# The last pass's sums inverted at full width, and the last tile stored in halves

## Chip, cores and metric

The kernel runs on one core of a Trainium2 chip. The metric is the device time of one execution in microseconds; lower is better. The inputs are bfloat16 and so is the output.

## What is computed

One block of attention whose output is gated, with a residual, over 2048 tokens of width 640. `x` is normalised (layer norm), and the result `xn` goes two ways:

```python
# attention: 32 heads of 20 columns
qkv = xn @ wqkv
p = softmax(q @ k.T * 20 ** -0.5)            # per head, 2048 x 2048
s = concat_heads(p @ v) @ wo
# gate: a gated pair of matrices (640 -> 1728 -> 640)
g = silu((sigmoid(xn @ w_gate) * (xn @ w_up)) @ w_down)
out = x + s * g
```

The part that matters here is the division in the softmax. The kernel does not divide the probabilities; it computes unnormalised sums `p @ v` together with the row sums of `p`, and divides the 20 columns of each head by the head's sum afterwards.

## The kernel before

**Passes.** The queries are cut into 4 chunks of 512 (`QC`), the heads into 8 groups of 4 (`NG`, `GH`). One pass handles one chunk and one group: for each of 16 key tiles and 4 heads TensorE computes a 128 x 512 block of scores (`score`, L1155), ScalarE takes the exponential of two or three blocks at once into `p` (L1177), VectorE takes that of some extra blocks by a cubic polynomial in four steps (`dve_exp`, L1188 to L1201; its scores lie in a bank named `spare`), and TensorE multiplies `p` with the values into `oacc` (`pv`, L1289). Each head has 32 rows of `oacc`: row 0 is the head's sum (the values carry a column of ones), rows 1 to 20 are its outputs.

**Order.** The order of all instructions on each engine is fixed when the program is built. A planner holds a clock for TensorE (`pe`), queues for ScalarE and VectorE (`act`, `dve`) with an assumed cost for each task, and cells that say when a result is there. Jobs are generators that ask for a free PSUM bank, emit matmuls and add VectorE tasks; two small banks (`misc0`, `misc1`, names `work` and `spare`) are shared by all jobs and by the extra score blocks. On the chip each engine runs its list in order and waits on semaphores.

**Normal division.** After an ordinary pass `normalise` copies `oacc` to `oev` (L772), sends the four sum rows through DRAM into a 128 x 16 tile `den`, inverts that (L782), sends it back through DRAM spread over each head's 32 rows (`rl`) and multiplies (L801), which gives `oT`, the operand of the output projection.

**The last pass** (chunk 3, group 7) is divided without that round trip. Its 512 queries are cut in two parts of 256 (`PARTS`), and each part's `oacc` columns are copied out as soon as they are complete (`take_part`, L815). The first part is divided in the job `last_job`, while the second part's scores still run; the second part is divided in the code at the end of the kernel, after everything else. Both do the same:

1. one matmul per 128 queries with `oev` as the stationary operand and `pick` as the moving one (L827, L1404) turns the four sums of each query into four columns; two such matmuls give 128 x 8 sums;
2. VectorE inverts the 128 x 8 values (L834, L1412) and copies each of them to 32 neighbouring columns, `rb` (L839, L1414);
3. one matmul per 128 queries with the fp32 identity `identf` (L847, L1416) turns `rb` back, so that each head's inverse stands in its 32 rows;
4. VectorE multiplies `oev` with that (L854, L1419) into `oT`.

**The output of the last chunk.** `part_job` has projected groups 0 to 5 of the last chunk beforehand, gated the result and added `x` (L751, L756; the sum with `x` by an accumulating DMA, L759), which gives `ahead`. What is left for each tile of 128 tokens are the matmuls of groups 6 and 7 (L866 for the first part, `out_mm`, L1393, for the second), a gate on each half of 320 columns (`gated`, L879, reads PSUM) and one addition of `gq_last` and `ahead` over 640 columns with the store of the tile (`summed`, L882 and L883). At the end of the kernel `keep_clock` (L1399) issues matmuls on zeros into a bank that nobody reads. The addition of the first part's last tile is kept in `later` and issued in the code at the end, behind the matmuls with `pick`. In the code at the end, gates and additions alternate: two gates and the addition of tile 2, then two gates and the addition of tile 3.

Of the kernel before, what the change touches and what calls it, by code (L numbers as in the profile page):

```python
# [9 lines left out]
FP32 = mybir.dt.float32  # L10
BF16 = mybir.dt.bfloat16
ACT = mybir.ActivationFunctionType
ALU = mybir.AluOpType
AXISX = mybir.AxisListType.X

P = 128
PARTS = ((0, 256), (256, 256))
HEAD = 32
GH = 4
NG = HEAD // GH  # L20
QC = 512
HALF = 320
# [6 lines left out]
OBUFS, WB = 1, 2  # L29
# [16 lines left out]
def kernel(  # L46
# [11 lines left out]
    nc = tc.nc  # L58
# [3 lines left out]
    S, D = x2.shape  # L62
# [6 lines left out]
    NQC = S // QC  # L69
# [7 lines left out]
    out_view = out2.rearrange("(p t) d -> p t d", t=TT)  # L77

    dram = ctx.enter_context(tc.tile_pool(name="dram", bufs=1, space=bass.MemoryType.DRAM))
    const = ctx.enter_context(tc.tile_pool(name="const", bufs=1))  # L80
# [15 lines left out]
    bound = const.tile([P, P], BF16, name="bound")  # L96
    heads = const.tile([P, DENSE, HEAD], BF16, name="heads")
    bounds = const.tile([P, DENSE, P], BF16, name="bounds")
    identf = const.tile([P, P], FP32, name="identf")
    pick = const.tile([P, GH], FP32, name="pick")  # L100
    zero = const.tile([P, P], BF16, name="zero")

    xnT = persist.tile([P, KD, S], BF16, name="xnT")
# [6 lines left out]
    wk = ctx.enter_context(tc.tile_pool(name="wk", bufs=2))  # L110
# [52 lines left out]
    with tc.tile_pool(name="setup", bufs=1) as sp, \  # L163
# [8 lines left out]
        sums = sp.tile([P, TT], FP32, name="sums")  # L172
# [183 lines left out]
        nc.gpsimd.memset(bounds, 0.0)  # L356
        nc.gpsimd.memset(v_all[:, :, VF:HEAD, 0:1], 1.0)
        nc.gpsimd.memset(wo_pad.rearrange("p g d -> p (g d)"), 0.0)
        make_identity(nc, identf)
        nc.gpsimd.memset(pick, 0.0)  # L360
        for j in range(GH):
            nc.gpsimd.memset(pick[32 * j:32 * j + 1, j:j + 1], 1.0)

    main = ExitStack()
    psum = main.enter_context(tc.tile_pool(name="psum", bufs=1, space=bass.MemoryType.PSUM,
# [6 lines left out]
    PE_OUT, SEM = 260.0, 70.0  # L372
# [37 lines left out]
    act, dve = Engine(), Engine()  # L410
    pe = [0.0]
# [38 lines left out]
    banks = [Cell(0.0), Cell(0.0)]  # L450
# [15 lines left out]
    def give_bank(held, cell):  # L466
        banks[held] = cell

    oTs, ot_cells, k_cells, q_cells, v_cells = {}, {}, {}, {}, {}
# [264 lines left out]
    gq_last, ahead = {}, []  # L734
# [72 lines left out]
    taken_parts, later = {}, []  # L807
# [11 lines left out]

    def last_job(u):  # L820
        q0, width = PARTS[u]
        part, n = taken_parts[u], width // P
        tiles = range(q0 // P, (q0 + width) // P)
        yield "wait", [part["cell"]]
        held, pd = yield "bank",
        for k in range(n):
            nc.tensor.matmul(pd[:, k * GH:(k + 1) * GH], lhsT=part["oev"][:, k * P:(k + 1) * P], rhs=pick,  # L827
                             start=True, stop=True, skip_group_check=True)
            yield "mm", 250.0, 0.0
        made = {}  # L830

        def invert():
            made["rq"] = wk.tile([P, n, GH], FP32, tag="den", bufs=2, name="rq")
            nc.vector.reciprocal(out=made["rq"].rearrange("p t j -> p (t j)"), in_=pd[:, 0:GH * n])  # L834

        def spread():
            made["rb"] = glu[0].tile([P, D], FP32, tag="gqr", bufs=4, name="rb")[:, 0:n * P].rearrange(
                "p (t j i) -> p t j i", t=n, j=GH)
            nc.vector.tensor_copy(out=made["rb"], in_=made["rq"].unsqueeze(3).to_broadcast([P, n, GH, 32]))  # L839

        cell = dve.add(160.0, [Cell(pe[0] + PE_OUT)], invert, -1)
        give_bank(held, cell)
        cell = dve.add(300.0, [cell], spread, -1)
        yield "wait", [cell]
        held, prl = yield "bank",
        for k in range(n):
            nc.tensor.matmul(prl[:, k * P:(k + 1) * P], lhsT=made["rb"][:, k, :, :].rearrange("p j i -> p (j i)"),  # L847
                             rhs=identf, start=True, stop=True, skip_group_check=True)
            yield "mm", 330.0, 200.0

        def scale():
            if steps[-1] not in oTs:
                oTs[steps[-1]] = wk.tile([P, QC], BF16, tag="oT", bufs=NG + 3, name="oT")
            nc.vector.tensor_tensor(out=oTs[steps[-1]][:, q0:q0 + width], in0=part["oev"], in1=prl[:, 0:width], op=ALU.mult)  # L854

        cell = dve.add(70.0 + width, [Cell(pe[0] + PE_OUT)], scale, -1)
        give_bank(held, cell)
        yield "known", lambda: all((NQC - 1) * 4 + t4 in out_cells for t4 in tiles)
        yield "wait", [cell, ot_cells[steps[-2]]]
        pair = glu[0].tile([P, D], FP32, tag="gqr", bufs=4, name="ot").bitcast(BF16)  # L860
        for t4 in tiles:
            got = []
            for h in range(2):
                held, ps = yield "bank",
                for g in range(NG - 2, NG):
                    nc.tensor.matmul(ps[:, 0:HALF], lhsT=oTs[NQC - 1, g][:, t4 * P:(t4 + 1) * P],  # L866
                                     rhs=wo_pad[:, g, h * HALF:(h + 1) * HALF], start=(g == NG - 2), stop=(g == NG - 1))
                    yield "mm", MM3
                got.append(dve.add(400.0, [Cell(pe[0] + PE_OUT)], lambda t4=t4, h=h, ps=ps: gated(t4, h, ps), 1))
                give_bank(held, got[-1])  # L870
            end = lambda t4=t4: summed(t4, pair[:, t4 % 2 * D:(t4 % 2 + 1) * D])
            if u == len(PARTS) - 2 and t4 == tiles[-1]:
                later.append(end)
            else:
                dve.add(740.0, [out_cells[(NQC - 1) * 4 + t4], *got], end, 2)

    def gated(t4, h, ps):
        gq = gq_last[t4][:, h * HALF:(h + 1) * HALF]
        nc.vector.scalar_tensor_tensor(out=gq, in0=ps[:, 0:HALF], scalar=0.25, in1=gq, op0=ALU.mult, op1=ALU.mult)  # L879

    def summed(t4, ot):
        nc.vector.tensor_tensor(out=ot, in0=gq_last[t4], in1=ahead[0][:, t4, :], op=ALU.add)  # L882
        nc.sync.dma_start(out=out_view[:, (NQC - 1) * 4 + t4, :], in_=ot)  # L883

    steps = [(qc, g) for qc in range(NQC) for g in range(NG)]
# [29 lines left out]
    for qc in range(NQC):  # L915
        parts = [[g for g in range(1, NG) if max(TILES[g]) == t] for t in range(5)] if not qc else [list(range(NG))]
        for groups in filter(None, parts):
            tiles = sorted({t for g in groups for t in TILES[g]})
# [8 lines left out]
    for h0, h1, n in V_PARTS:  # L927
        for t in range(0 if h0 else V_SETUP, TT, n):
            tiles = list(range(t, min(t + n, TT)))
# [20 lines left out]
    glu = []  # L950
# [363 lines left out]
    for t, a in ((4, 4 * Dh), (5, 0)):  # L1314
        for k in range(2):
            row, j = a + k * Dh, 2 * (t - 4) + k
# [3 lines left out]
    while pv_pass[0] < len(steps) - 1 + len(PARTS):  # L1320
# [5 lines left out]
        p = min(b0, NB - 1) // PER_PASS  # L1326
        until, stuck, can = 1e18, False, False
        if b0 < NB:
# [13 lines left out]
            if can and (until <= pe[0] + (0.0 if mode[0] == "score" else 40.0) or idle):  # L1342
                idle = False
                n = issue()
# [4 lines left out]
        held = sum(len(q) for q in ready_p)  # L1349
# [32 lines left out]
    qc, g = steps[-1]  # L1382
    q0, width = PARTS[-1]
    tiles = range(q0 // P, (q0 + width) // P)
    units = [(t4, h) for t4 in tiles for h in range(2)]
    oev = taken_parts[len(PARTS) - 1]["oev"]
    main.close()
    ending = ctx.enter_context(tc.tile_pool(name="ending", bufs=1, space=bass.MemoryType.PSUM))
    banks = [ending.tile([P, 512], FP32, tag=f"end{k}", name="last") for k in range(2 * QC // P)]
    banks, pd, prl, unused = banks[1:1 + len(units)], banks[6], banks[7], banks[0]  # L1390

    def out_mm(bank, t4, h, gg):
        nc.tensor.matmul(bank[:, 0:HALF], lhsT=oTs[qc, gg][:, t4 * P:(t4 + 1) * P],  # L1393
                         rhs=wo_pad[:, gg, h * HALF:(h + 1) * HALF],
                         start=(gg == NG - 2), stop=(gg == NG - 1), skip_group_check=True)

    def keep_clock(n):
        for _ in range(n):
            nc.tensor.matmul(unused, lhsT=zero, rhs=xnT[:, 0, 0:512], start=True, stop=True, skip_group_check=True)  # L1399

    for bank, (t4, h) in zip(banks[:-1], units):
        out_mm(bank, t4, h, NG - 2)
    for k, t4 in enumerate(tiles):
        nc.tensor.matmul(pd[:, k * GH:(k + 1) * GH], lhsT=oev[:, k * P:(k + 1) * P], rhs=pick,  # L1404
                         start=True, stop=True, skip_group_check=True)
    for end in later:
        end()
    out_mm(banks[-1], *units[-1], NG - 2)
    keep_clock(2)
    n = len(tiles)  # L1410
    rq = wk.tile([P, n, GH], FP32, tag="den", bufs=2, name="rq")
    nc.vector.reciprocal(out=rq.rearrange("p t j -> p (t j)"), in_=pd[:, 0:GH * n])  # L1412
    rb = wk.tile([P, n, GH, 32], FP32, tag="rl", bufs=OBUFS, name="rb")
    nc.vector.tensor_copy(out=rb, in_=rq.unsqueeze(3).to_broadcast([P, n, GH, 32]))  # L1414
    for k, t4 in enumerate(tiles):
        nc.tensor.matmul(prl[:, k * P:(k + 1) * P], lhsT=rb[:, k, :, :].rearrange("p j i -> p (j i)"), rhs=identf,  # L1416
                         start=True, stop=True, skip_group_check=True)
    keep_clock(2)
    nc.vector.tensor_tensor(out=oTs[qc, g][:, q0:], in0=oev, in1=prl[:, 0:width], op=ALU.mult)  # L1419
    pair = glu[0].tile([P, D], FP32, tag="gqr", bufs=4, name="ot").bitcast(BF16)  # L1420
    for bank, (t4, h) in zip(banks, units):
        out_mm(bank, t4, h, NG - 1)
        gated(t4, h, bank)
        if h == 1:
            summed(t4, pair[:, t4 % 2 * D:(t4 % 2 + 1) * D])
# [1 line left out]
_INS = ['A_x', 'A_wqkv', 'A_wo', 'B_x', 'B_w_gate', 'B_w_up', 'B_w_down']  # L1427
_OUTS = [((1, 2048, 640), 'bfloat16')]
# [25 lines left out]
```

## Time and profile before

| | |
|---|---|
| median of 3 runs | 894.33 us (893.8 to 894.76) |
| the profiled execution | 894.27 us, span of its instructions 892.1 us |
| ScalarE (ACT) busy | 870.6 us, 98% of the span |
| VectorE (DVE) busy | 840.7 us, 94% |
| TensorE (PE) busy | 804.6 us, 90% |
| GpSimd (POOL) busy | 162.0 us, 18% |
| granted TensorE clock, mean | 0.998 |

The span runs from the first to the last instruction; the rest of the execution's time, 2.2 us, lies around it. Start times in the views count from the start of the span. A row of the groups gives the line of the kernel, the engine, the operation, the tiles that it writes and reads with their shapes, how often it ran, its busy time in us, the mean of one in ns, and the idle time of the engine before it with what ended it. In the chain of waits each piece has its start, its length in us, the engine and the line. A VectorE operation's length reaches some 0.08 us into the next one's: 512 columns take 0.68 us and follow each other at 0.60.

### The profile page before, as it was taken

The numbers are of one execution on the slowest core, as the hardware profiler recorded it, in microseconds if no ns is written. First come the engines' busy times: TensorE is split into PE (matmuls) and PEld (weight loads), VectorE is DVE, ScalarE is ACT, GpSimd is POOL, SyncE is SP. The second block draws the span as 40 slices with busy tenths as digits, with TensorE's granted clock in tenths as the row PEclk, the third lists the DMA queues.
The fourth block names the chain that finished last, engine by engine and source line by source line (L and its number), as shares of the span: only waits on it lengthen the run. The fifth ranks groups of instructions, "written<-read, shape, count | busy, mean of one in ns | idle before, by whom it ended". The sixth has DMA issues, their size and how long they took to land.

```text
span 892.1 us, 16911 instructions
## 1 busy us (share of the span) xinstructions
PE 804.6 (90%) x6227; PEld 290.3 (33%) x6310; DVE 840.7 (94%) x1487; ACT 870.6 (98%) x837; POOL 162.0 (18%) x305
## 2 busy tenths in 40 slices
PE   5899899998999999999899998989999898999896
PEld 3344333332223333232233332223333332233333
DVE  7799999999999999997999999999999989999997
ACT  6999999999999999999999999999999999999995
POOL 7401111111111212111101221101112220111121
PEclk9999999999999999999999999999999999999999
DMA  8113231135451234223212243313113432200012
GB/s 317 46 35 90 64 109 35 52 98 150 109 133 42 64 89 69 65 59 72 64 23 79 70 81 79 71 26 77 34 45 85 108 54 70 67 17 21 14 32 71
DMA packets 107672, 64.40 MB, mean 72 GB/s; under 512 B 80350, under 2 KB 101906, under 8 KB 107498
## 3 DMA queue, kind: packets, MB, share of 16 engines
q1 hardware_dynamic: 97382, 47.21, 19.8%
q0 software_dynamic: 10208, 16.11, 8.2%
q8 instruction: 49, 0.80, 0.4%
q14 instruction: 33, 0.27, 0.1%
HBM read 50.45 MB, written 16.13 MB: 75 GB/s over the span
## 4 chain that ended last, share of the span: by engine, by line
ACT 64%; issue 18%; PE 10%; DVE 7%; DMA 0%; SPq 0%; DVEq 0%; ACTq 0%
ACT p L1177 59%; PE sc L1155 3%; ACT tnh L651 3%; PE oacc L1289 2%; DVE dy L1188 2%; PE work L644 1%; DVE du L1193 1%; PE work L124 1%; PE work L680 1%; ACT td L691 1%; DVE stats L227 1%; DVE p L1201 1%; DVE du L1197 1%; PE work L150 1%; DMA x_sb<-in_A_x_dram 0%
## 5 line engine op out<-in xcount | busy, mean ns | idle before, releaser
L1177 ACT ACTIVATE p<-sc 128x1536 bf16<-128x1536 f32 x717 | 827.9, 1358 | 2.0 <-PE oacc L1289 1.4
L1155 PE MATMUL sc<-qT,kT_all 21*128 21x512 bf16 (+1 forms) x1848 | 280.0, 375 | 57.4 <-ACT p L1177 49.3
L1188 DVE TENSOR_SCALAR dy<-spare 128x512 f32<-128x512 f32 x257 | 175.6, 683 | 22.9 <-PE spare L1155 20.2
L1155 PEld LDWEIGHTS <-kT_all 21*128 21x128 bf16 x2112 | 91.0, 91 | 286.6 <-issue 274.6
L1197 DVE SCALAR_TENSOR_TENSOR du<-du,dy 128x512 f32<-128x512 f32 x257 | 174.4, 682 | 1.7
L1201 DVE SCALAR_TENSOR_TENSOR p<-du,dy 128x512 uint16<-128x512 f32 x257 | 174.2, 680 | 1.4
L1193 DVE SCALAR_TENSOR_TENSOR du<-dy 128x512 f32<-128x512 uint16 x257 | 174.4, 682 | 0.8
L1289 PE MATMUL oacc<-p,v_all 128*21 128x512 bf16 (+1 forms) x2112 | 157.3, 376 | 0.6 <-DVE v_all L157 0.3
L1155 PE MATMUL spare<-qT,kT_all 21*128 21x512 bf16 (+1 forms) x264 | 98.6, 378 | 0.0
L773 POOL DMA_DIRECT2D den_dram<-oev x31 | 18.0, 579 | 391.5 <-DVE oev L772 391.5
L680 PE MATMUL work<-wd,hT 128*128 128x320 bf16 x448 | 85.5, 302 | 0.1
L644 PE MATMUL work<-xnT,wg 128*128 128x512 bf16 (+1 forms) x261 | 77.6, 383 | 1.9 <-issue 0.8
L657 PE MATMUL work<-xnT,wu 128*128 128x512 bf16 (+1 forms) x268 | 73.1, 381 | 1.2 <-DVE dy L1188 0.3
L789 POOL DMA_DIRECT2D rl<-rec_dram x124 | 62.0, 512 | 57.7 <-DMA rec_dram<-den 48.0
L1265 PE MATMUL oacc<-xnT,zero 128*128 128x512 bf16 x165 | 56.0, 384 | 3.4 <-issue 2.5
L1289 PEld LDWEIGHTS <-v_all 128*21 128x21 bf16 x2112 | 31.1, 90 | 62.0 <-issue 60.1
L680 PEld LDWEIGHTS <-hT 128*128 128x128 bf16 x448 | 35.0, 97 | 48.6 <-issue 39.1
L651 ACT ACTIVATE tnh<-work 128x512 bf16<-128x512 f32 (+1 forms) x56 | 41.2, 735 | 0.0
L661 DVE SCALAR_TENSOR_TENSOR hT<-tnh,work 128x512 bf16<-128x512 bf16 (+1 forms) x56 | 37.9, 678 | 2.2 <-ACT tnh L651 2.2
L783 POOL DMA_DIRECT2D rec_dram<-den x31 | 17.0, 547 | 120.0 <-DVE den L782 115.3
L719 PE MATMUL work<-wo_pad,oT 128*128 128x320 bf16 x192 | 35.6, 302 | 0.5 <-issue 0.5
L644 PEld LDWEIGHTS <-wg 128*128 128x128 bf16 (+1 forms) x280 | 21.7, 98 | 42.8 <-issue 31.1
(123 smaller groups left out, 553.6 us busy)
## 6 DMA issues: line engine op xcount, KB each, us to landing
wg<-in_B_w_gate_dram SPq DMA_DIRECT2D x52, 160.0 KB
wu<-in_B_w_up_dram SPq DMA_DIRECT2D x52, 160.0 KB
rl<-rec_dram POOLq DMA_DIRECT2D x124, 64.0 KB, 2.5
qT<-q_dram SPq DMA_DIRECT2D x31, 128.0 KB
gq_dram<-d POOLq DMA_DIRECT2D x12, 320.0 KB, 2.5
gqr<-gq_dram SPq DMA_DIRECT2D x12, 320.0 KB
kT_all<-k_dram SPq DMA_DIRECT2D x28, 128.0 KB
wd<-in_B_w_down_dram SPq DMA_DIRECT2D x13, 160.0 KB
```

The lines of the kernel that those rows point to most:

```text
L644: nc.tensor.matmul(psg[0:fsz, :], lhsT=wg[:, kd, 0:fsz], rhs=xnT[:, kd, cols], start=(kd == 0), stop=(kd == KD - 1))
L651: nc.scalar.activation(out=made["t"][0:fsz, :], in_=psg[0:fsz, :], func=ACT.Tanh, scale=0.5)
L657: nc.tensor.matmul(psu[0:fsz, :], lhsT=wu[:, kd, 0:fsz], rhs=xnT[:, kd, cols], start=(kd == 0), stop=(kd == KD - 1))
L680: nc.tensor.matmul(psd[:, 0:HALF], lhsT=hT[0:fsz, kf, t4 * P:(t4 + 1) * P], rhs=glu[1][0:fsz, kf, e0_:e1_], start=(kf == 0), stop=(kf == N ...
L789: nc.gpsimd.dma_start(out=t["rl"][32 * j:32 * j + 32, :], in_=rec_dram[n, j:j + 1, :].to_broadcast([32, QC]))
L1155: nc.tensor.matmul(ps[:, c0:c0 + n], lhsT=kT_all[rows, g, kt * P:(kt + 1) * P], rhs=qTs[qc, g][rows, q0:q0 + n], start=True, stop=True, ti ...
L1177: nc.scalar.activation(out=buf.tile(), in_=ps, func=ACT.Exp, bias=EXP_BIAS, scale=exp_scale)
L1188: nc.vector.tensor_scalar(out=t["y"], in0=ps, scalar1=LEAST, scalar2=None, op0=ALU.max)
L1193: nc.vector.scalar_tensor_tensor(out=t["u"], in0=t["f"], scalar=CUBE_2, in1=t["f"], op0=ALU.add, op1=ALU.mult)
L1197: nc.vector.scalar_tensor_tensor(out=t["u"], in0=t["u"], scalar=CUBE_1, in1=t["f"], op0=ALU.add, op1=ALU.mult)
L1201: nc.vector.scalar_tensor_tensor(out=buf.tile()[:, 0, :].bitcast(U16), in0=t["u"], scalar=CUBE_SCALE, in1=t["y"], op0=ALU.mult, op1=ALU.add)
L1289: nc.tensor.matmul(oacc[32 * j:32 * j + 1 + Dh, q0:q0 + width], lhsT=v_all[:, kt, GH * g + j, 0:1 + Dh], rhs=buf.ap[:, i, c0:c0 + width], ...
```

## The change

The four steps of the division become three in both places: one fp32 matmul with a constant `spread` (row 32j holds ones in columns 32j to 32j+31) puts each head's sum into all of its 32 rows, 128 x 256 at once; VectorE inverts these 128 x 256 values out of PSUM; VectorE multiplies with `oev`. In the planner the VectorE task of `last_job` is one task with a cost of 652 ns, in place of tasks with 160, 300 and 326 ns. In the code at the end the four gates come first and the additions after them, in halves of 320 columns: the first half of tile 2 is added by GpSimd, the other three by VectorE. Tile 2 is stored whole, tile 3 in two halves. Of the constants, `identf` and `pick` go and `spread` comes. Two times two filler matmuls (`keep_clock`) become three.

```diff
--- before.py
+++ after.py
@@ -96,8 +96,7 @@
     bound = const.tile([P, P], BF16, name="bound")
     heads = const.tile([P, DENSE, HEAD], BF16, name="heads")
     bounds = const.tile([P, DENSE, P], BF16, name="bounds")
-    identf = const.tile([P, P], FP32, name="identf")
-    pick = const.tile([P, GH], FP32, name="pick")
+    spread = const.tile([P, P], FP32, name="spread")
     zero = const.tile([P, P], BF16, name="zero")
 
     xnT = persist.tile([P, KD, S], BF16, name="xnT")
@@ -356,10 +355,9 @@
         nc.gpsimd.memset(bounds, 0.0)
         nc.gpsimd.memset(v_all[:, :, VF:HEAD, 0:1], 1.0)
         nc.gpsimd.memset(wo_pad.rearrange("p g d -> p (g d)"), 0.0)
-        make_identity(nc, identf)
-        nc.gpsimd.memset(pick, 0.0)
+        nc.gpsimd.memset(spread, 0.0)
         for j in range(GH):
-            nc.gpsimd.memset(pick[32 * j:32 * j + 1, j:j + 1], 1.0)
+            nc.gpsimd.memset(spread[32 * j:32 * j + 1, 32 * j:32 * j + 32], 1.0)
 
     main = ExitStack()
     psum = main.enter_context(tc.tile_pool(name="psum", bufs=1, space=bass.MemoryType.PSUM,
@@ -819,41 +817,21 @@
 
     def last_job(u):
         q0, width = PARTS[u]
-        part, n = taken_parts[u], width // P
+        part = taken_parts[u]
         tiles = range(q0 // P, (q0 + width) // P)
         yield "wait", [part["cell"]]
-        held, pd = yield "bank",
-        for k in range(n):
-            nc.tensor.matmul(pd[:, k * GH:(k + 1) * GH], lhsT=part["oev"][:, k * P:(k + 1) * P], rhs=pick,
-                             start=True, stop=True, skip_group_check=True)
-            yield "mm", 250.0, 0.0
-        made = {}
-
-        def invert():
-            made["rq"] = wk.tile([P, n, GH], FP32, tag="den", bufs=2, name="rq")
-            nc.vector.reciprocal(out=made["rq"].rearrange("p t j -> p (t j)"), in_=pd[:, 0:GH * n])
-
-        def spread():
-            made["rb"] = glu[0].tile([P, D], FP32, tag="gqr", bufs=4, name="rb")[:, 0:n * P].rearrange(
-                "p (t j i) -> p t j i", t=n, j=GH)
-            nc.vector.tensor_copy(out=made["rb"], in_=made["rq"].unsqueeze(3).to_broadcast([P, n, GH, 32]))
-
-        cell = dve.add(160.0, [Cell(pe[0] + PE_OUT)], invert, -1)
-        give_bank(held, cell)
-        cell = dve.add(300.0, [cell], spread, -1)
-        yield "wait", [cell]
-        held, prl = yield "bank",
-        for k in range(n):
-            nc.tensor.matmul(prl[:, k * P:(k + 1) * P], lhsT=made["rb"][:, k, :, :].rearrange("p j i -> p (j i)"),
-                             rhs=identf, start=True, stop=True, skip_group_check=True)
-            yield "mm", 330.0, 200.0
+        held, sums = yield "bank",
+        nc.tensor.matmul(sums[:, 0:width], lhsT=spread, rhs=part["oev"], start=True, stop=True)
+        yield "mm", 700.0, 500.0
 
         def scale():
             if steps[-1] not in oTs:
                 oTs[steps[-1]] = wk.tile([P, QC], BF16, tag="oT", bufs=NG + 3, name="oT")
-            nc.vector.tensor_tensor(out=oTs[steps[-1]][:, q0:q0 + width], in0=part["oev"], in1=prl[:, 0:width], op=ALU.mult)
-
-        cell = dve.add(70.0 + width, [Cell(pe[0] + PE_OUT)], scale, -1)
+            over = glu[0].tile([P, D], FP32, tag="gqr", bufs=4, name="over")[:, 0:width]
+            nc.vector.reciprocal(out=over, in_=sums[:, 0:width])
+            nc.vector.tensor_tensor(out=oTs[steps[-1]][:, q0:q0 + width], in0=part["oev"], in1=over, op=ALU.mult)
+
+        cell = dve.add(140.0 + 2 * width, [Cell(pe[0] + PE_OUT)], scale, -1)
         give_bank(held, cell)
         yield "known", lambda: all((NQC - 1) * 4 + t4 in out_cells for t4 in tiles)
         yield "wait", [cell, ot_cells[steps[-2]]]
@@ -1387,7 +1365,12 @@
     main.close()
     ending = ctx.enter_context(tc.tile_pool(name="ending", bufs=1, space=bass.MemoryType.PSUM))
     banks = [ending.tile([P, 512], FP32, tag=f"end{k}", name="last") for k in range(2 * QC // P)]
-    banks, pd, prl, unused = banks[1:1 + len(units)], banks[6], banks[7], banks[0]
+    banks, sums, unused = banks[1:1 + len(units)], banks[7], banks[0]
+
+    def total(engine, t4, h, pair):
+        cols = slice(h * HALF, (h + 1) * HALF)
+        engine.tensor_tensor(out=pair[:, t4 % 2 * D:(t4 % 2 + 1) * D][:, cols], in0=gq_last[t4][:, cols],
+                             in1=ahead[0][:, t4, cols], op=ALU.add)
 
     def out_mm(bank, t4, h, gg):
         nc.tensor.matmul(bank[:, 0:HALF], lhsT=oTs[qc, gg][:, t4 * P:(t4 + 1) * P],
@@ -1400,29 +1383,27 @@
 
     for bank, (t4, h) in zip(banks[:-1], units):
         out_mm(bank, t4, h, NG - 2)
-    for k, t4 in enumerate(tiles):
-        nc.tensor.matmul(pd[:, k * GH:(k + 1) * GH], lhsT=oev[:, k * P:(k + 1) * P], rhs=pick,
-                         start=True, stop=True, skip_group_check=True)
+    nc.tensor.matmul(sums[:, 0:width], lhsT=spread, rhs=oev, start=True, stop=True, skip_group_check=True)
     for end in later:
         end()
     out_mm(banks[-1], *units[-1], NG - 2)
-    keep_clock(2)
-    n = len(tiles)
-    rq = wk.tile([P, n, GH], FP32, tag="den", bufs=2, name="rq")
-    nc.vector.reciprocal(out=rq.rearrange("p t j -> p (t j)"), in_=pd[:, 0:GH * n])
-    rb = wk.tile([P, n, GH, 32], FP32, tag="rl", bufs=OBUFS, name="rb")
-    nc.vector.tensor_copy(out=rb, in_=rq.unsqueeze(3).to_broadcast([P, n, GH, 32]))
-    for k, t4 in enumerate(tiles):
-        nc.tensor.matmul(prl[:, k * P:(k + 1) * P], lhsT=rb[:, k, :, :].rearrange("p j i -> p (j i)"), rhs=identf,
-                         start=True, stop=True, skip_group_check=True)
-    keep_clock(2)
-    nc.vector.tensor_tensor(out=oTs[qc, g][:, q0:], in0=oev, in1=prl[:, 0:width], op=ALU.mult)
+    keep_clock(3)
+    over = glu[0].tile([P, D], FP32, tag="gqr", bufs=4, name="over")[:, 0:width]
+    nc.vector.reciprocal(out=over, in_=sums[:, 0:width])
+    nc.vector.tensor_tensor(out=oTs[qc, g][:, q0:], in0=oev, in1=over, op=ALU.mult)
     pair = glu[0].tile([P, D], FP32, tag="gqr", bufs=4, name="ot").bitcast(BF16)
     for bank, (t4, h) in zip(banks, units):
         out_mm(bank, t4, h, NG - 1)
         gated(t4, h, bank)
-        if h == 1:
-            summed(t4, pair[:, t4 % 2 * D:(t4 % 2 + 1) * D])
+        if t4 == tiles[0] and h == 0:
+            total(nc.gpsimd, t4, h, pair)
+    for t4, h in units[1:]:
+        total(nc.vector, t4, h, pair)
+        if t4 == tiles[-1]:
+            nc.sync.dma_start(out=out_view[:, (NQC - 1) * 4 + t4, h * HALF:(h + 1) * HALF],
+                              in_=pair[:, t4 % 2 * D + h * HALF:t4 % 2 * D + (h + 1) * HALF])
+        elif h == 1:
+            nc.sync.dma_start(out=out_view[:, (NQC - 1) * 4 + t4, :], in_=pair[:, t4 % 2 * D:(t4 % 2 + 1) * D])
```

## The prediction

> **What bounds the kernel now.** I read the page first: ScalarE is busy 870.6 of 892.1 us, VectorE 840.7, TensorE 804.6. That is an average over 892 us. The change touches some 20 us at the end, and the built order of the changed program is the same as before up to the first matmul of `last_job`, at about 870.8 us, apart from constants that GpSimd fills near 33 us while nothing waits for it. So the end decides, and there I read the chain of waits piece by piece (start, us, what):
>
> ```profile
> 875.21 0.78 ACT p L1177
> ...
> 881.91 0.43 DVE oev L815
> 882.38 0.57 PE last L1393 x3
> 882.95 0.35 PE last L1404 x4
> 883.38 0.22 DVE rq L1412
> 883.63 0.30 DVE rb L1414
> 883.98 0.73 PE last L1416 x4
> 884.73 0.43 DVE oT L1419
> 885.20 0.73 PE last L1393 x4
> ...
> 888.13 0.82 DVE ot L882
> ```
>
> Two stretches are to be seen. Up to 881.4 us ScalarE sets the pace (the timeline has its last nine calls without a gap from 871.64 to 881.40). From 881.91 on it is one thread: every piece waits for the one before, and all that it loses or saves reaches the end. The sums take it from 882.34 (`oev` copied) to 885.16 (`oT` scaled), 2.82 us. Gates and additions take it from 885.55 to 888.95, 3.40 us; then the last store is issued and 2.8 us of landing and closing follow:
>
> ```profile
> 888.98 0.33 SPq L883 DMA_DIRECT2D out_dram<-ot  x1
> ```
>
> The first part's sums (`last_job`) lie in the first stretch, in a VectorE queue without gaps. The timeline there (start, length):
>
> ```profile
> 872.27 0.20 DVE L834 RECIPROCAL rq<-work 128x8 f32<-128x8 f32 x1
> 872.39 0.43 DVE L756 SCALAR_TENSOR_TENSOR hT<-work,kT_all 128x320 f32<-128x320 f32 x1
> 872.75 0.28 DVE L839 COPY rb<-rq 128x256 f32<-128x256 f32 x1
> ```
>
> **The price that decides: a reciprocal of 256 columns.** The trace has none. By shape, the groups (mean ns) show
>
> ```profile
> L782 DVE RECIPROCAL den<-den 128x16 f32<-128x16 f32 x31 | 7.5, 242 | 0.0
> L241 DVE RECIPROCAL rstd<-rstd 128x1 f32<-128x1 f32 x8 | 1.2, 146 | 0.5 <-ACT rstd L237 0.2
> L1419 DVE TENSOR_TENSOR oT<-oev,last 128x256 bf16<-128x256 f32 x1 | 0.4, 422 | 0.8 <-PE last L1416 0.8
> L834 DVE RECIPROCAL rq<-work 128x8 f32<-128x8 f32 x1 | 0.2, 197 | 0.0
> ```
>
> An ordinary VectorE operation grows by about 1.02 ns a column (422 ns at 256, 684 at 512). A reciprocal grows from 197 ns at 8 columns to 243 at 16, that is 5.75 ns a column; start to next start it is 0.12 against 0.17 us, 6.25 ns. I take 5.75, since it compares two operations run in the same way, back to back: R = 0.243 + 240 x 0.00575 = 1.62 us. Bounds: the 208 ns of L1412 against 243 give 4.4 ns and R = 1.30; the shortest at one column (109) against the longest at 16 (248) give 9.3 ns and R = 2.47; if the growth in small rows is only a start-up, R is the 0.42 of L1419.
>
> **Part 1, the last sums (the thread).** Removed: two matmuls with `pick`, the 8-column reciprocal, the copy `rb`, two matmuls with `identf`. Added: one matmul and R. From the end of `oev`: 0.04 to TensorE, 0.41 for three output matmuls (882.38 to 882.79), the new matmul, 0.08 to VectorE, R, 0.04, the multiplication 0.42. The new fp32 matmul streams the same 256 columns as the two of L1416 (0.73 in the chain) with half the weight loads; the four-column ones of L1404 take 0.50. Between those ends I take 0.65, nearer the one with equal columns. Sum 1.64 + R = 3.26 against 2.82: **+0.44**. `later`'s addition (0.81) still fits under the matmuls. One more filler matmul has TensorE idle beside it and costs nothing; without that idle time, 0.2.
>
> **Part 2, the first part's sums (`last_job`).** VectorE loses 0.12 (reciprocal), 0.19 (copy, start to start) and 0.33 (multiplication, at 877.61), and gains R and the multiplication directly behind it. The reciprocal starts at 872.27 as before, because VectorE is not free sooner and its matmul is done by 871.5. It ends at 873.89, the multiplication at 874.34, and the half of `part_job` (L756) that ran at 872.39 runs from 874.27 to 874.75. Two things wait, because the order of TensorE is fixed: the extra scores ("spare") need the bank that the reciprocal reads, and three output matmuls behind them need the bank that this half frees. Before, both were free by 872.9. Now the three run from 874.81 and the score group behind them from 875.21, done at 875.60; before it was issued at 874.53 and the ScalarE call that reads it started at 875.21. The call starts at 875.65: 0.45 late, in a ScalarE without gaps. Later `oT` of the group before (L801) ends at 878.75, and the last `dy` chain at 879.35; TensorE waits for both ahead of a score group, another 0.1. Together **+0.55**; for other R it is R - 1.07, and about 0.05 where R is small (then only the longer matmul is left). VectorE's idle 0.72 us at 878.4 does not help, as the delay is already in ScalarE's queue.
>
> **Part 3, gates and additions.** Before: four gates of 0.40 and two additions of 0.74 start to start, with two waits. Now gates and three half additions follow each other at 0.40 (a 320-column operation); from the first gate's start to the last addition's end 6 x 0.40 + 0.48 = 2.88 instead of 3.40: **-0.52**. The fourth half is GpSimd's. No GpSimd row has two inputs; its 128x640 row (L246) takes 0.88, so 320 columns lie between 0.44 and, at double per column, 0.88; at worst twice that. I take 0.8. It starts 0.52 after the first gate's start, and VectorE's first addition 1.60 after, so 1.08 us cover it.
>
> Here the trace shows a conflict: VectorE's tiny operation with two SBUF inputs (L242) takes 0.16 us alone and 0.59 and 0.65 at 8.71 and 20.76 us, in which GpSimd's L246 runs. [...]
>
> **Part 4, the last store.** The windows show its packets moving for 0.62 us (889.80 to 890.42) for 160 KB, 128 packets of 1280 bytes. A half has 128 packets of 640 bytes, so the gain lies between 0 and 0.31. SP issues three stores at 0.33 each, 0.40 apart, and that fits; the store ahead may still move packets for 0.1. I take **-0.20**. Behind SP's wait for GpSimd's half stand the two last stores.
>
> **Sum.** 0.44 + 0.55 - 0.52 - 0.20 = +0.27 us on the profiled execution's 894.27 (span 892.1 and 2.2 around it), 0.06 below the median of the runs: 894.54, say **894.6**. In terms of R: 2R - 2.97 above R = 1.1.
>
> **Rivals.** (A) the forecast, R between 1.3 and 2.1: 893.9 to 895.5. Chance 0.62.
> (B) Slower: a steep reciprocal, R above 2.1. At 9.3 ns a column R is 2.47; part 2 then costs 1.40 and part 1 1.29, and the time is 896.2. It stands twice on the path, and from R = 2.38 (8.9 ns) on the sum passes 0.2%. For it: the one-column rows. Against it: 8 to 16 columns, by length and by start. Chance 0.13.
> [...]
> (C) Faster: the small rows show a start-up and wide reciprocals stream like a copy, R = 0.42. Then 0.05 - 0.76 - 0.72 = -1.43: 892.8. Against: one-column reciprocals (146) are no slower than other small operations. Chance 0.08.
> (D) The first part's delay is hidden, as ScalarE's queue had more slack than its starts show: +0.44 - 0.72, 894.0. For it: VectorE idles at 878.4. Chance 0.11.
> (E) GpSimd's half is late: beyond 1.08 us every excess holds VectorE's additions and SP's stores. At 1.76 us it costs 0.7 (895.2), and it passes 0.2% from about 2.6 us on. Chance 0.06.
> That the change doesn't do what it says is not among them: the built order shows each part.
>
> **Numbers.** 0.2% is 1.79 us, about what a measurement of this kernel can tell from no change. A, D and most of C lie within it (C's far side: 0.04 faster); half of B and most of E lie beyond (0.12 slower). The range goes from just above C, 893.0, to B, 896.2, and leaves out about 0.16.
>
> **What would show it.** Right: reciprocals of 1.3 to 2.2 us at the two new lines, a ScalarE call near 875.2 about 0.45 late, 3.0 to 3.8 us from `oev`'s end to the last `oT`, 2.9 from the first gate to the last addition, GpSimd's half under 1.1. Wrong: a reciprocal of 0.4 or over 2.4; ScalarE's last call ending at 881.4 as before; an addition that waits for GpSimd; a part of the program before 870 us that moves.

## The result, and the profile after

The changed kernel takes 904.77 us (median of 4 runs, 903.16 to 905.55) against 894.22 for the kernel before: a ratio of 1.0113, 95% interval 1.0101 to 1.0124. It is slower by 10.5 us, where the prediction's sum was +0.27. The profiled run took 905.55 us, with a span of 903.56 and a mean granted clock of 0.986; before, the span was 892.10 and the clock 0.998. It is the slowest of the four runs: the time goes with the clock, and the fastest had 0.993.

The chain of waits of the changed kernel (start, us, what):

```profile
872.32 1.68 DVE over L831
...
874.04 0.38 PE spare L1133 x2
874.42 0.55 PE oacc L1267 x16
874.96 0.89 PE work L749 x3
...
877.97 1.46 ACT p L1155
...
886.06 0.44 DVE oev L813
...
888.44 1.77 DVE over L1392
...
890.23 0.43 DVE oT L1393
...
893.54 0.40 DVE ot L1372
```

Set this beside the chain before, piece by piece. Starts and lengths are those of the single instructions, so the terms add up to the whole difference of the spans, 11.46 us:

| stretch | before, us | after, us | difference | forecast |
|---|---|---|---|---|
| up to the start of the last part's `oev` copy | 881.91 | 886.06 | +4.14 | +0.55 |
| from there to the end of the last `oT` | 3.23 | 4.60 | +1.37 | +0.44 |
| from there to the first gate | 0.40 | 0.40 | 0.00 | 0 |
| first gate's start to last addition's end | 3.40 | 2.89 | -0.52 | -0.52 |
| last addition's end to the last store's issue | 0.03 | 0.16 | +0.13 | in the -0.20 |
| last store's issue to the span's end | 3.12 | 9.45 | +6.33 | -0.20 |

The first and the last row hold most of what was not foreseen; the second holds another 0.93. The reciprocals themselves are not the cause. The groups of VectorE near the end (busy us, mean ns of one):

```profile
L1392 DVE RECIPROCAL over<-last 128x256 f32<-128x256 f32 x1 | 1.8, 1758 | 1.2 <-PE last L1386 1.2
L831 DVE RECIPROCAL over<-work 128x256 f32<-128x256 f32 x1 | 1.8, 1751 | 0.0
```

R is 1.75, against 1.62 forecast; that changes the sum by 0.26 and no more.

**The first row.** The windows of TensorE, cut every 3.41 us so that each change of the granted clock falls on a cut (length; then PE, PEld, DVE, ACT, POOL busy us; PEclk; DMA share; GB/s). First the window of the kernel before in which its small reciprocal runs, then the changed kernel:

```profile
871.34:874.75 3.41, 3.20 (x44) 1.57 (x41) 3.28 (x8) 3.41 (x4) 0.10 (x1) 1.00 0.37 100
```

```profile
868.13:871.54 3.41, 2.83 (x41) 1.39 (x41) 3.36 (x7) 3.41 (x4) 2.25 (x4) 1.00 0.42 91
871.54:874.95 3.41, 2.37 (x37) 1.03 (x32) 3.38 (x6) 3.41 (x4) 0.64 (x2) 1.00 0.25 82
874.95:878.37 3.42, 3.42 (x32) 1.17 (x32) 3.32 (x7) 1.96 (x3) 0.23 (x1) 0.50 0.00 0
...
885.19:888.61 3.42, 2.89 (x23) 1.68 (x16) 1.70 (x4) 0.00 (x0) 0.00 (x0) 0.50 0.27 93
```

Before the clock falls there is one window in which TensorE is busy 2.37 of 3.41 us (3.20 in the kernel before); then it runs at half speed for 13.65 us, four such windows. The hole in that window is the work of the reciprocal. The waits of TensorE between 870 and 889 us (in all, times, longest):

```profile
PE sc L1133 <- ACT p L1155: 0.7, 1, 0.7
...
PE spare L1133 <- DVE over L831: 0.4, 1, 0.4
```

The three output matmuls (L749) that filled the wait for ScalarE before, at 872.52, now stand behind the extra score block, which waits for the reciprocal: two waits follow each other with little between. At half speed three output matmuls take 0.89 us in the chain instead of 0.57, and ScalarE, which had no gap before, waits for scores. The timeline of ScalarE in the kernel before and in the changed one:

```profile
869.40 11.99 ACT L1177 ACTIVATE p<-sc 128x1536 bf16<-128x1536 f32 x11
```

```profile
869.37 6.12 ACT L1155 ACTIVATE p<-sc 128x1536 bf16<-128x1536 f32 x5
876.50 1.02 ACT L1155 ACTIVATE p<-sc 128x1024 bf16<-128x1024 f32 x1 [1.01 <-PE sc L1133]
877.97 3.86 ACT L1155 ACTIVATE p<-sc 128x1536 bf16<-128x1536 f32 x3 [0.45 <-PE sc L1133]
882.36 1.02 ACT L1155 ACTIVATE p<-sc 128x1024 bf16<-128x1024 f32 x1 [0.52 <-PE sc L1133]
883.89 0.60 ACT L1155 ACTIVATE p<-sc 128x512 bf16<-128x512 f32 x1 [0.51 <-PE sc L1133]
```

In the changed kernel's trace the granted clock changes at 874.95, 888.61 and 892.02 us. The first two lie some 13.65 us apart, the last two 3.41: four of these windows and one.

**The last row.** What the closing of the program waited for, from SP's queue of the changed kernel:

```profile
SPq L1430 <- PEq L1430: 7.2, 2, 6.7
...
SPq L1430 <- DMA out_dram<-ot: 1.1, 2, 0.7
```

The stores are waited for 1.1 us; 7.2 go to another engine's close (before, 1.3 and 0.7). PE is named, but it had long been done: its last matmul ended by 891.5. It is GpSimd: the instructions at the program's closing line, before and then after (ns min/median/max, first and last start):

```profile
L1449 POOLq DRAIN  x3: 51/102/11132, 878.7 to 891.8; - x3
```

```profile
L1430 POOLq DRAIN  x3: 51/102/11104, 891.7 to 903.3; - x3
```

The first of the three drains, 11.1 us long, starts with GpSimd's last instruction. Before, that is the DMA at L759 (878.73), and the drain is over at 889.84, before the last store has landed (890.42). In the changed kernel it is the half addition (891.69), and the drain is over at 902.77.

### The profile page after: what moved, and what is told of

Read it like the earlier page. It is cut to its first block, busy times and chain, and to the rows that moved or that the text cites. A ratio compares the mean times of both kernels' runs of the same rounds, so it can differ in the third digit from the quotient of the medians.

```text
span 903.6 us, 16885 instructions
## 1 busy us (share of the span) xinstructions
PE 808.9 (90%) x6215; PEld 290.3 (32%) x6298; DVE 843.7 (93%) x1486; ACT 871.2 (96%) x837; POOL 162.8 (18%) x304
## 4 chain that ended last, share of the span: by engine, by line
ACT 62%; issue 17%; PE 11%; DVE 7%; DMA 1%; SPq 0%; DVEq 0%; ACTq 0%
ACT p L1155 57%; PE sc L1133 4%; ACT tnh L649 3%; PE oacc L1267 2%; DVE dy L1166 2%; PE work L642 1%; DVE du L1171 1%; PE work L123 1%; DVE p L1179 1%; ACT td L689 1%; DVE stats L226 1%; DVE du L1175 1%; PE work L678 1%; PE work L149 1%; PE work L655 0%
```

## Experiments

Two theories: **half clock** (the reciprocal's wait empties a window of TensorE, the clock falls to half and the scores come late) and **late GpSimd** (GpSimd closes a fixed time behind its last instruction, so any work near the end shows). Rivals: the waits alone cost the time; the new small stores close slowly. Each kernel was run beside the kernel before, whose medians were 894.28, 894.43 and 894.36 in the three groups of runs (e1 to e4; e5 to e8; e2b, e9, e11).

**e1: the changed kernel, all four half additions on VectorE.**

```diff
-        if t4 == tiles[0] and h == 0:
-            total(nc.gpsimd, t4, h, pair)
-    for t4, h in units[1:]:
+    for t4, h in units:
```

> The changed kernel, with the one half addition of GpSimd given to VectorE; everything else stays, the half stores and the first part's sums too. Theory 'late GpSimd' (GpSimd needs some 11.1 us between its last instruction and its close, so an instruction at 891.7 puts the end at 902.8): the last store to the span's end shrinks from 9.49 to about 3.1 us, one more addition costs 0.40, so 904.8 - 6.4 + 0.4 = about 898.8 us. Rival 'small stores' (the half rows of 640 bytes, or three stores instead of two, close slowly): the 9.5 us stay and the time is about 905.

Median 897.70 us of 5 runs: 895.23, 896.34, 897.70, 898.74, 900.34. In the profiled run the last store's issue to the span's end is 2.94 us (892.86 to 895.80) with the half stores still there: the rival of the small stores falls. The runs are far apart, and their mean clock goes with the time: 0.998 for the fastest, 0.989 for the slowest.

**e2 and e2b: the kernel before, with one tiny copy on GpSimd** whose result nobody reads, behind the second gate (e2) or behind the last `oev` copy (e2b).

```diff
         gated(t4, h, bank)
+        if t4 == tiles[0] and h == 0:
+            nc.gpsimd.tensor_copy(out=eps_t, in_=gq_last[t4][:, 0:1])
```

```diff
     keep_clock(2)
+    nc.gpsimd.tensor_copy(out=eps_t, in_=oev[:, 0:1])
     n = len(tiles)
```

> The kernel before, with one more GpSimd instruction: a copy of one column, which waits for the second gate of the last part and whose result nobody reads. Theory 'late GpSimd': the copy ends near 886.2 on the scale of the profile before, the close of GpSimd comes 11.1 us later, at 897.3, and the span ends 0.8 behind that, at 898.1 instead of 892.1: +6.0, about 900.2 us. Rival 'small stores': nothing in the stores has changed and the copy delays nobody: 894.2. Rival 'the addition itself' (a two-input operation of 320 columns is what GpSimd is slow to finish): also 894.2.

> The kernel before, with the one-column copy on GpSimd placed earlier: it waits for the last oev copy (near 882.4 on the scale of the profile before) instead of the second gate (886.0). Theory 'late GpSimd', with the number of e2_late_gpsimd and of the kernels before and after: GpSimd's closing drain ends 10.2 us behind the end of its last instruction, whatever that is (879.64 to 889.84, 886.72 to 896.94, 892.55 to 902.77), and the span ends 0.8 to 1.1 behind that. Copy done at 882.6, drain at 892.8, span 893.7 instead of 892.1: about 895.9 us. Rival 'any GpSimd work behind the last DMA costs its 5 us': 899.6 again. Rival 'a copy this small is free': 894.3.

e2: 899.61 us (899.38 to 899.97), ratio 1.0058 [1.0043, 1.0073]. e2b: 896.35 us (895.66 to 896.58), ratio 1.0020 [1.0010, 1.0029]. In e2 the copy sits behind the first gate of tile 2, not the second as the expectation says. GpSimd's timeline in e2, in e2b and in the changed kernel:

```profile
886.54 0.19 POOL L1425 COPY eps_t<-kT_all 128x1 f32<-128x1 f32 x1 [6.56 <-DVE kT_all L879]
```

```profile
882.66 0.62 POOL L1410 COPY eps_t<-oev 128x1 f32<-128x1 f32 x1 [2.84 <-DVE oev L815]
```

```profile
891.69 0.86 POOL L1372 TENSOR_TENSOR ot<-kT_all,hT 128x320 bf16<-128x320 f32 x1 [12.64 <-issue]
```

The long drains end at 896.94, 893.49 and 902.77: 10.2 us behind the end of that instruction in all three, and 10.2 behind the end of the DMA instruction of the kernel before (879.64 to 889.84). Which of these three kinds of instruction it is makes no difference; a copy of one column costs 5.3 us, and one that ends 3.4 us earlier costs 2.0. So the rival in e2b's expectation, a fixed price for any GpSimd work behind the last DMA, falls. The sizes expected held within 0.6 us. In e2b the copy takes 0.62 instead of 0.19: VectorE's addition with two SBUF inputs runs from 882.42 to 883.23, and the copy ends right behind it, at 883.28. In e2 the copy ran from 886.54 to 886.73 beside gates, with one input in PSUM (885.89 to 886.78), and took the 0.19.

**e3: the kernel before, with the first part's sums alone done the new way** (the new `last_job` and the constant `spread`; the setup's identity is kept in the setup's own pool to make room).

> The kernel before, with only the first part's sums done the new way (one matmul, the reciprocal of 256 columns and the multiplication in last_job); the end is the old one. Theory 'half clock' (the two waits behind the reciprocal, 0.68 and 0.35 us, let the granted clock of TensorE fall to half for four windows of 3.41 us, and the scores that ScalarE reads are then late): the last oev copy at about 886 instead of 881.9, and the end, whose first matmuls are still at half rate, some 0.3 more: about 898.4 us, with windows of a clock of 0.5. Rival 'waits alone' (ScalarE loses only the delay of one call, and what else went was the end's): +0.6 to 0.7, about 894.9.

Median 898.71 us of 7 runs, in two groups: 895.20, 895.40, 895.45 at a mean clock of 0.998, and 898.71, 898.77, 899.07, 899.22 at 0.990 to 0.992. The profiled run is one of the upper group; its windows:

```profile
872.71:876.12 3.41, 2.38 (x34) 1.06 (x34) 3.38 (x5) 3.02 (x3) 0.12 (x1) 1.00 0.17 48
876.12:879.53 3.41, 3.30 (x35) 0.96 (x33) 3.41 (x7) 3.01 (x3) 0.91 (x1) 0.50 0.02 5
```

Again 2.38 us of matmuls, and half rate behind them. So the same program costs 1.1 us or 4.7, as the clock holds or falls. Neither expectation had the two groups; each names one of them. The kernel before has such runs too: of its 75 here, two took 897.6 and 897.7, at a mean clock of 0.992.

**e4 and e9: the kernel before, with the end alone done the new way**, on VectorE only; in e9 with eight fillers during the last reciprocal.

```diff
-    keep_clock(3)
+    keep_clock(8)
     over = glu[0].tile([P, D], FP32, tag="gqr", bufs=4, name="over")[:, 0:width]
     nc.vector.reciprocal(out=over, in_=sums[:, 0:width])
```

> The kernel before, with only the end done the new way (one matmul, the reciprocal of 256 columns, gates first, four half additions all on VectorE, the last tile stored in halves); the first part's sums are the old ones. Both main theories: the prediction's part 1 with a reciprocal of 1.75 instead of 1.62 is +0.57, part 3 with a fourth addition -0.12, part 4 -0.20: +0.25, about 894.5 us, full clock up to 882, close 3.1 us. Rival 'small stores': about 900.5. Rival 'the one wide matmul lets the clock fall by itself, at the end': the multiplication of oT 0.5 us and more later than that sum, 895.2 or above.

> e4_end_new_vector with eight fillers in place of three while VectorE inverts the last part's sums, so that of the 1.58 us that TensorE waited there about 0.5 is left. Theory 'half clock at the end too' (the runs of e4 at 895.7 to 896.5 had a mean clock of 0.996, those at 894.0 to 895.1 one of 0.997 to 0.998): every run at 894.0 to 895.1. Rival 'spread of the close' (the upper runs come from the last store or the engines' closing): the same two groups as e4.

e4: median 894.93 us of 10 runs, six at 894.03 to 895.12 and four at 895.74 to 896.50, with mean clocks of 0.997 to 0.998 and 0.996. e9: 894.72 us, all ten at 894.37 to 895.12. TensorE's waits at the end, e4 and then e9:

```profile
PE last L1402 <- DVE oT L1419: 1.6, 1, 1.6
```

```profile
PE last L1402 <- DVE oT L1419: 0.5, 1, 0.5
```

With the hole filled the upper group is gone. That fits a fall of the clock behind the last reciprocal too, at a smaller price, since little of the program is left to slow down. It is not shown directly: the profiled run of e4 is one of the lower group, and its clock holds to the end of the matmuls.

**e5: e3 with three fillers** in front of the score group for which TensorE waits 0.68 us.

```diff
+        if split and after_sums and after_sums[0] == 1:
+            after_sums[0] = 2
+            for _ in range(3):
+                nc.tensor.matmul(oacc, lhsT=zero, rhs=xnT[:, 0, 0:QC], start=False, stop=False, skip_group_check=True)
         for i, b in enumerate(taken):
             score(ps[:, i, :], b)
```

> e3_first_part_new with three matmuls on zeros (512 columns each, added to oacc, which they leave as it is) in front of the scores for which TensorE waits 0.68 us at about 873. Each streams for some 0.21 us, so they fit into that wait and should delay nothing. Theory 'half clock': the window that held 2.38 us of matmuls now holds about 3.0, the clock stays full in every run, and every run is as the three of e3_first_part_new whose mean clock was 0.998: 895.2 to 895.5 us. Rival 'waits alone' (the delays and not the clock are what costs, and e3's two groups of times have another cause): no change, some runs again at 898.7 to 899.2, or 0.6 above that if the fillers delay the scores.

895.26 us, all ten runs at 895.14 to 895.89, clock 0.997 to 0.999. The two windows of the place where e3 fell, and ScalarE's timeline:

```profile
870.16:873.58 3.42, 3.29 (x35) 1.32 (x28) 3.37 (x6) 3.42 (x4) 2.02 (x4) 1.00 0.68 152
873.58:876.99 3.41, 2.93 (x40) 1.28 (x40) 3.38 (x7) 2.99 (x4) 0.00 (x0) 1.00 0.06 20
```

```profile
869.79 6.12 ACT L1162 ACTIVATE p<-sc 128x1536 bf16<-128x1536 f32 x5
876.33 6.15 ACT L1162 ACTIVATE p<-sc 128x1024 bf16<-128x1024 f32 x6 [0.42 <-PE sc L1140]
```

Nothing about the reciprocal, its waits or its dependencies has changed; TensorE only works on zeros while it waits. Of the four gaps that ScalarE had in e3's profile one is left, of 0.42 us. None of the ten runs is above 895.9, where e3 had four of seven at 898.7 to 899.2. Theory half clock is shown, and the rival "waits alone" falls.

**e6: e3 with the planner told 2090 ns for the task**, in place of 652.

```diff
-        cell = dve.add(140.0 + 2 * width, [Cell(pe[0] + PE_OUT)], scale, -1)
+        cell = dve.add(2090.0, [Cell(pe[0] + PE_OUT)], scale, -1)
```

> e3_first_part_new, but the planner is told 2090 ns for the task of the first part's sums instead of 652. The built order then has no extra score block behind that reciprocal (ScalarE takes its columns, 0.4 to 0.5 us), and the output matmuls stand behind the next score group with a filler ahead of them. Theory 'half clock': with no wait of TensorE behind the reciprocal the clock stays full; the time is 894.3 plus 0.2 to 1.0 for ScalarE's extra columns and the later multiplication, 894.5 to 895.3 us. Rival 'the order has no better place': the output matmuls that are moved back leave the same window as empty, the clock falls in some runs, 898 and more.

894.82 us (894.63 to 895.49), ratio 1.000 [0.9991, 1.0009], clock 0.997 to 0.999 in ten runs. This is as expected. The planner's order avoids the fall by itself: the changed kernel's order was made for a reciprocal and multiplication of 0.65 us that take 2.2.

**e7: the kernel before, with gates first, half additions on VectorE and the last tile stored in halves**, the sums as they were.

> The kernel before, with only the cheap parts of the change: the four gates first, then four half additions on VectorE, the last tile stored in two halves. The sums are the old ones in both places and GpSimd gets nothing. From the trace of e4_end_new_vector: gates and additions 3.30 instead of 3.40 us, last issue to SP's drain 2.16 instead of 2.29, but 0.11 in which SP is still issuing the store ahead: -0.1 us, 894.2, not to be told from before. If the halves are worth what the prediction said (-0.12 - 0.20) 893.95. Rival 'small stores': 895 or more.

894.32 us (11 runs, 893.65 to 894.83), ratio 0.9998 [0.9989, 1.0007]: no difference that can be told. This is the cheap half of the change; nothing in these runs beats the kernel before.

**e8 and e11: the changed kernel without GpSimd's addition and with the fillers of e5**; e11 with eight fillers at the end as well.

> e1_vector_adds_all (the changed kernel without GpSimd's half addition) with the three fillers of e5_fillers: both suspected costs taken away, all else as changed. Both main theories together: 2R - 2.97 with R = 1.75 is +0.53, the fourth addition on VectorE +0.40: about 895.2 us in every run, where e1 spread from 895.23 to 900.34, clock 0.997 or more. If the clock has another cause at the end of the kernel (behind 882 us, where TensorE waits for the last reciprocal), some runs are still 1 to 2 us above.

> e8_fillers_no_gpsimd with eight fillers in place of three at the end: the changed kernel with no GpSimd addition and with TensorE busy in both waits. Theory 'half clock': every run at 895.0 to 895.5 (895.2 by the prediction's sum with R = 1.75 and a fourth addition on VectorE), none at 896 to 898 as e8 had three of ten. Rival 'spread of the close': some runs again above 896.

e8: 895.66 us, ten runs at 895.09 to 898.18, three of them over 896. e11: 895.58 us, all ten at 895.47 to 895.88, ratio 1.0013 [1.0004, 1.0023]. The fillers at the end take away the upper runs here too. That these were falls of the clock stays argued: two of the three had a mean clock of 0.998, like the fast runs. With both unforeseen costs taken out, the change is 1.2 us slower than before, a little above the 895.0 to 895.5 expected.

## Why the prediction was wrong

**Part 2, the first part's sums: the step that failed by most on the path of the work.** It found the waits that the profile then showed: the reciprocal starts at 872.24 (872.27 forecast), the three matmuls run from 874.96 in the chain (874.81), and ScalarE is held up once at that place (0.42 in e5, 0.45 forecast). It priced them as a delay in a queue, +0.55. It took every matmul behind them at the duration of before, and that was the error: the two waits left a window of TensorE with 2.37 us of matmuls, and 13.65 us ran at half rate. From the start of that reciprocal to the last `oev` copy the changed kernel takes 13.82 us, where the same work takes 10.69 at full clock (e8): the fall cost 3.1 us there, and 0.8 more in the last sums. No step or rival looked at the clock, although the windows of before have the column, and the code has fillers named `keep_clock`. Without the fall the step was low by less. With R = 1.75 it gives 0.68; e5 costs 0.83 between medians (895.26 - 894.43), and within the traces the 10.69 us of e5, e8 and e11 stand against 9.64 for the old sums: +1.04. ScalarE's last call ends 0.70 later, as the step has it. The other 0.34 comes behind that call: VectorE has no gap from 870.51 to 877.74 in e5's chain and makes TensorE wait 0.2 us for the group before's `oT`, where 0.1 was allowed, and from there the chain runs through the output matmuls and no longer through ScalarE.

**Part 3, the half on GpSimd: right in what it priced, wrong in what it left out.** Gates and additions take 2.89 us, as forecast; GpSimd's half takes 0.86 (0.8 forecast) inside its cover of 1.08. The step asked only who waits for the result. The close of the program waits for the engine, 10.2 us behind its last instruction, and the trace before had that row. It is the largest single part: 6.33 of the profile's 11.46 us.

**Part 1, the last sums: the size was nearly right, at full clock.** From the end of `oev` to the end of `oT` e4 takes 3.36 us against 2.82, +0.54 where +0.44 was forecast; 0.13 of it is R. In the changed kernel it is 4.18, since its output and sum matmuls still ran at half rate.

**R: nearly right.** 1.75 us is 6.3 ns a column on top of the 16-column row's 0.243; the prediction read 6.25 from start to start, and took 5.75. Rival C's stream (0.42) is out.

**Part 4, the half store: mis-sized.** In e4 the last issue to SP's drain takes 2.11 us against 2.28 before, but the last store is issued 0.12 behind the last addition (0.03 before), as SP still issues the one ahead; about 0.1 is left of the 0.20.

**Rivals.** E named the right instruction, but its mechanism (VectorE's additions wait for the half) and its price (0.7) were others; the addition was early enough, ending at 892.55, and VectorE's first one started at 892.66. B, C and D were not what happened. With e11 the prediction's own sum can be judged: 2R - 2.97 is +0.53 at R = 1.75, and +0.40 for the fourth addition on VectorE makes 0.93; measured, 1.22.

**Open.** What makes the granted clock fall. A window of 2.37 or 2.38 us of matmuls was followed by half rate in the changed kernel, e1 and e3; one of 2.27 in e6 (880.47 to 883.88) was not. Nor were emptier ones at the end, of other matmuls: 1.77 us in e4 (883.08 to 886.49), and 1.81 in e1 itself:

```profile
885.17:888.59 3.42, 1.81 (x13) 0.96 (x9) 2.91 (x3) 0.00 (x0) 0.00 (x0) 1.00 0.14 48
888.59:892.00 3.41, 0.72 (x4) 0.31 (x4) 2.98 (x8) 0.00 (x0) 0.00 (x0) 1.00 0.00 0
```

So no threshold of busy time follows from these traces; that the waits cause the fall rests on the fillers of e5. Why half rate lasts three windows or four is open as well. Nor is it shown why three of e3's seven runs kept the clock. The author's estimate is that the windows' place against the hole differs from run to run, as it does between two traces: half rate begins 2.63 us behind the reciprocal's start in the changed kernel (872.32 to 874.95) and 3.57 behind it in e3 (872.55 to 876.12). Only one run of each kernel has a trace.

## What to carry to other kernels

A wait of a TensorE that runs beside the path was not free here: a window with 1.04 us of gaps was followed by 13.65 us at half rate. So before lengthening a VectorE operation that a matmul waits for, look at the waits that it gives TensorE and at the granted clock behind them, try fillers in the wait, and tell a planner the true cost. GpSimd's last instruction set when the program could close here, 10.2 us behind its end, so look in the profile at how long an engine's closing drain takes before giving it work near the end. When the runs of one kernel fall into two groups, read the mean clock of each before averaging them; it also counts the idle close at half rate (11.5 us in the changed kernel, from 892.02 on), so compare runs of one kernel alone.

## What the runs showed of the hardware

GpSimd's closing drain ended 10.2 us behind the end of its last instruction, be that a DMA issue (the kernel before), a copy of one column (0.19 us in e2, 0.62 in e2b) or an addition of 320 (0.86 us, the changed kernel). The granted clock changed on a grid of 3.41 us (874.95, 888.61 and 892.02 in the changed kernel), and a window with about 1.0 us of gaps was followed by 10.2 us (e1) or 13.65 us (the changed kernel, e3) of half rate, though emptier ones at the end of e1 (1.81 us busy) and e4 (1.77) were not. An fp32 reciprocal out of PSUM took 1.75 us for 256 columns. Three matmuls of 512 columns on zeros took away some 3.5 us (the median of e3 against that of e5).
